# An adaLN block on one core: the second half's down projection as one deep Strassen product

## The chip, the cores and the metric

One core of a Trainium2 chip runs the whole kernel. The metric is device time in microseconds; a profile of one execution gives what each engine did when. TensorE (PE, with its weight loads PEld) multiplies into banks of PSUM, VectorE (DVE) and ScalarE (ACT) read and write PSUM and SBUF, GpSimd (POOL) works on SBUF, and SyncE's queue (SP) issues the DMAs.

## The reference

An adaptive layer norm block on x of 2048 tokens by 512 features, all in float32:

```python
x = x + ga * _A_ref(h, A_wqkv, A_wo)          # linear attention, 32 heads of 16
h = _layernorm(x, axis=-1) * (1 + cb) + sb
g = jnp.einsum("bsd,df->bsf", x, w_gate)      # 512 x 1376
u = jnp.einsum("bsd,df->bsf", x, w_up)        # 512 x 1376
h = g * u
return jnp.einsum("bsf,fd->bsd", h, w_down)   # 1376 x 512
x = x + gb * _B_ref(h, B_w_gate, B_w_up, B_w_down)
```

In `_B_ref` the argument x is the normalized h. The change touches only the last part: the gated product h = g u and its down projection, for half of the tokens.

## The kernel before, in words

**Precision.** Every float32 operand of a matmul is split into a high part in the faster format fp32r and a low part, the rest. A product is three matmuls: high by high, high by low, low by high. The splitting is one copy on ACT (high) and one subtraction on DVE or POOL (low), L196 and L197 in `split`.

**Tiling.** The tokens are four chunks of 512 (four tiles of 128 each, index j), the 1376 hidden features 11 tiles f (ten of 128, and f = 10 of 96). The feed-forward part works on pairs of chunks, (0, 1) and then (2, 3).

**Blocks.** For a pair of chunks and one f, `block` makes g and u of both chunks, a 2x2 by 2x2 block product (chunk and half of the contraction by half of the contraction and gate or up), by Strassen and Winograd's scheme: seven products instead of eight. Each is six matmuls of 128x512 (`times`, L1132), so a block is 42. Four PSUM banks a, b, c, d hold the running sums. ACT copies a bank into another or into SBUF (L1137), DVE adds bank c to p5 after product 5 (L1191) and bank d to u2 after product 6 (L1195), and multiplies g by u for either chunk at the end (`mul`, L1160): the first of these reads bank a, the second bank c. A product can be written to a bank only when the readers of what stood in it are done: product 7 writes bank c after the add of L1191, product 1 of the next block writes bank a. With `aside` a copy of bank a is multiplied; the second pair runs without it.

**Beside the blocks.** `block` is a generator with seven points, after product 1 "p1", 2 "p5", 3 "p6", 4 "p2", 5 "p7", 6 "p3", 7 "p4"; what hangs on a point is issued there, behind whatever its engine has already. These are the loads (L1094) and, on POOL, sums (L1100) and lows (L1118) of the gate and up weights of later blocks, with their highs on ACT (L1111, L1114), the scaling of w_down by gb on DVE (L1277), the split of w_down, the split of h (L196, L197), and work for later chunks by the table `plan`.

**Down projection.** f tiles are taken in groups; `groups` lists for (2, 3): (10, 0, 1), (2, 3, 4), (5, 6, 7), (8, 9). When a group's blocks are through, its matmuls (L1212, L1213, L1214: for each f and token tile high-high, high-low, low-high of 512 columns) are cut into parts, and one part, a down group, is issued after each of the next blocks; DVE adds the result to x (`evac`, L943), and for the last group SP stores it (L945). The last group comes after the last block, its last token tile as two halves of 256 columns. Instructions run in the order in which they are written, engine by engine; a tile framework adds the waits.

## Time and profile before

| what | value |
|---|---|
| median of three runs | 545.67 us (545.53 to 545.91) |
| span of the profiled execution | 543.5 us; 2.2 us less than the median |
| PE busy | 537.6 us, 99% of the span |
| DVE, ACT, POOL busy | 382.4, 293.7, 204.0 us |
| second pair | from 363.67 us to the end |
| one block | 42 matmuls, 9.5 us |

Rows of the timeline read: start in us, duration in us, engine, line, operation, output <- inputs, shapes, count, and in brackets how long the engine had been idle and what released it. Rows of groups read: count, then busy us and mean ns of one, then idle time before them. A matmul row's duration (0.39) is longer than its share of the stream, since matmuls are pipelined; the distance of two starts is what one costs.

### The profile page before, as it was taken

What the parts mean: (1) busy time and instruction counts of PE and PEld (TensorE: products, weight loads), DVE (VectorE), ACT (ScalarE), POOL (GpSimd) and SP (SyncE); (2) the same over time, 40 slices, a digit from 0 to 9 for tenths busy, and PEclk for the clock granted to TensorE, in tenths of its full rate; (3) what the DMA queues carried; (4) which work ended last, traced back from release to release, by engine and by line L of the source; (5) the groups of instructions that cost most, each with busy time, mean ns of one, the idle gap of its engine ahead of it and who ended that gap; (6) DMA issues with size and microseconds to landing.
All of it is one profiled execution on the core that took longest, in us unless ns stands there. A gap on an engine that the chain in (4) does not pass through costs nothing.

```text
span 543.5 us, 7368 instructions
## 1 busy us (share of the span) xinstructions
PE 537.6 (99%) x2419; PEld 441.3 (81%) x2419; DVE 382.4 (70%) x638; ACT 293.7 (54%) x546; POOL 204.0 (38%) x207
## 2 busy tenths in 40 slices
PE   8999999999999999999999999999999999999997
PEld 7888787888888878878888888877888888888885
DVE  7997779999989878769776568985453443444444
ACT  3696776657578765577665545444442344444210
POOL 2001010010021220094896566766666656446100
PEclk9999999999999999999999999999999999999999
DMA  8903326310166165856262151982343222200004
GB/s 285 386 26 112 122 102 209 109 47 2 59 180 206 34 215 168 271 147 184 82 182 86 47 185 40 304 244 63 117 118 92 58 59 59 59 19 1 0 0 157
DMA packets 68455, 65.65 MB, mean 121 GB/s; under 512 B 8448, under 2 KB 46592, under 8 KB 68416
## 3 DMA queue, kind: packets, MB, share of 16 engines
q1 hardware_dynamic: 68416, 65.17, 38.4%
q8 instruction: 19, 0.31, 0.2%
q14 instruction: 20, 0.16, 0.1%
HBM read 46.27 MB, written 18.87 MB: 120 GB/s over the span
## 4 chain that ended last, share of the span: by engine, by line
PE 94%; DVE 3%; SPq 1%; issue 1%; DMA 0%; ACT 0%; DVEq 0%
PE bank L1132 33%; PE acc L873 8%; PE acc L1212 6%; PE acc L1214 6%; PE acc L1213 6%; PE bank L211 4%; PE bank L209 3%; PE bank L210 3%; PE acc L416 2%; PE acc L418 2%; PE bank L958 2%; PE bank L956 2%; PE acc L417 2%; PE bank L957 2%; PE acc L146 2%; SPq L334 1%
## 5 line engine op out<-in xcount | busy, mean ns | idle before, releaser
L1132 PE MATMUL bank<-h,w 128*128 128x512 f32 (+1 forms) x798 | 184.0, 389 | 0.0
L1132 PEld LDWEIGHTS bank<-h,w 128*128 128x128 f32 (+1 forms) x798 | 148.5, 186 | 32.6 <-DVE u L1191 0.2
L1137 ACT ACTIVATE bank<-bank 128x512 f32<-128x512 f32 (+1 forms) x38 | 22.2, 583 | 138.5 <-PE bank L1132 138.3
L943 DVE TENSOR_TENSOR x<-acc,x 128x512 f32<-128x512 f32 (+1 forms) x73 | 48.5, 680 | 49.0 <-PE acc L1214 47.3
L1118 POOL TENSOR_TENSOR w<-raw,w 128x256 fp32r<-128x256 f32 (+3 forms) x38 | 40.4, 1064 | 89.0 <-ACT w L1111 84.9
L197 POOL TENSOR_TENSOR w<-raw,w 128x512 fp32r<-128x512 f32 (+1 forms) x26 | 36.3, 1400 | 65.6 <-ACT w L196 59.9
L1212 PE MATMUL acc<-w,kh 128*128 128x512 f32 (+2 forms) x154 | 59.6, 387 | 0.0
L1213 PE MATMUL acc<-w,kh 128*128 128x512 f32 (+2 forms) x154 | 59.6, 387 | 0.0
L1214 PE MATMUL acc<-w,kl 128*128 128x512 f32 (+2 forms) x154 | 59.5, 386 | 0.0
L265 POOL TENSOR_TENSOR rstd<-ve,half 128x2 f32<-128x2 f32 (+3 forms) x13 | 11.6, 889 | 108.5 <-DVE ve L264 46.0
L1118 POOL TENSOR_TENSOR w<-t,w 128x512 fp32r<-128x512 f32 (+1 forms) x38 | 49.6, 1325 | 0.0
L197 DVE TENSOR_TENSOR kl<-u,kh 128x512 fp32r<-128x512 f32 (+1 forms) x38 | 26.4, 735 | 30.2 <-ACT kh L196 30.2
L211 PE MATMUL bank<-w,h 128*128 128x512 f32 x104 | 40.9, 394 | 0.1
L209 PE MATMUL bank<-w,h 128*128 128x512 f32 x104 | 40.9, 393 | 0.0
L210 PE MATMUL bank<-w,h 128*128 128x512 f32 x104 | 40.6, 390 | 0.0
L873 PE MATMUL acc<-w,xh 128*128 128x512 f32 x120 | 37.1, 390 | 0.0
L1191 DVE TENSOR_TENSOR u<-bank,u 128x512 f32<-128x512 f32 (+1 forms) x19 | 13.1, 688 | 31.3 <-PE bank L1132 23.7
L1212 PEld LDWEIGHTS acc<-w,kh 128*128 128x128 f32 (+1 forms) x154 | 28.9, 188 | 6.0
L1213 PEld LDWEIGHTS acc<-w,kh 128*128 128x128 f32 (+1 forms) x154 | 28.9, 188 | 5.9
L1214 PEld LDWEIGHTS acc<-w,kl 128*128 128x128 f32 (+1 forms) x154 | 28.9, 188 | 5.9
L1100 POOL TENSOR_TENSOR t<-raw,t 128x256 f32<-128x256 f32 (+1 forms) x34 | 25.8, 759 | 2.0 <-DMA raw<-in_B_w_up_dram 0.7
L873 PEld LDWEIGHTS acc<-w,xh 128*128 128x128 f32 x120 | 22.5, 188 | 4.6
(224 smaller groups left out, 1102.2 us busy)
## 6 DMA issues: line engine op xcount, KB each, us to landing
raw<-in_w_mod_dram SPq DMA_DIRECT2D x24, 256.0 KB, 4.0
raw<-in_B_w_down_dram SPq DMA_DIRECT2D x20, 256.0 KB, 3.1
raw<-in_B_w_gate_dram SPq DMA_DIRECT2D x36, 128.0 KB, 3.5
raw<-in_B_w_up_dram SPq DMA_DIRECT2D x36, 128.0 KB, 3.5
x<-in_A_x_dram SPq DMA_DIRECT2D x16, 256.0 KB, 5.4
out_dram<-x SPq DMA_DIRECT2D x15, 256.0 KB, 2.7
moved<-h SPq DMA_DIRECT2D x14, 256.0 KB, 2.2
u<-moved SPq DMA_DIRECT2D x56, 64.0 KB, 2.0
```

The lines of the kernel that those rows point to most:

```text
L197: (low or nc.vector).tensor_tensor(l, src, f32(h), op=ALU.subtract)
L209: nc.tensor.matmul(ps, ah, bh, start=i == 0, stop=False)
L210: nc.tensor.matmul(ps, ah, bl, start=False, stop=False)
L211: nc.tensor.matmul(ps, al, bh, start=False, stop=i == n - 1)
L873: nc.tensor.matmul(yps[i], x, y, start=False, stop=k == KD - 1 and x is al, skip_group_check=True)
L943: nc.vector.tensor_tensor(xt[:, a:b], dn[j][:, a:b], xt[:, a:b], op=ALU.add)
L1100: sub = lambda out, x, y: (on or nc.gpsimd).tensor_tensor(out, x, y, op=ALU.subtract)
L1118: sub = lambda out, x, y: (on or nc.gpsimd).tensor_tensor(out, x, f32(y), op=ALU.subtract)
L1132: mm = lambda x, y, **kw: nc.tensor.matmul(ps, x[:, k], y, skip_group_check=True, **kw)
L1212: nc.tensor.matmul(ps, hh[:, a:b], dh[:n, c:d], start=i == 0, stop=False)
L1213: nc.tensor.matmul(ps, hh[:, a:b], dl[:n, c:d], start=False, stop=False)
L1214: nc.tensor.matmul(ps, hl[:, a:b], dh[:n, c:d], start=False, stop=i == len(hs) - 1)
```

## The change

The four groups of the second pair go. Its 11 blocks run first, with f = 10 first and h kept whole for f = 0 to 9 (`raw`: no split at the end of a block). The first three of them are still followed by the down groups left over from the first pair. Then `Down.run` makes the down projection of both chunks in one: the ten tiles f = 0 to 9 are five pairs, and for a pair, h of two chunks by two tiles times w_down of two tiles by two halves of 256 columns is again a 2x2 by 2x2 product done in seven. The sums over the five pairs stay in PSUM, so that each of the seven products is, for each token tile j, five accumulated pairs. f = 10 is added as an ordinary product (`odd_product`).

The high and low parts of a half of w_down lie side by side in one tile of 512 columns, so that h high by both is one matmul of 512 columns (L1404), and h low by w high one of 256 (L1405); the two halves of the bank are added when it is read (`both`, or `taken`, whose first half is an ACT copy).

The four sums of w_down per pair (`w_sum`, L1352), its scaling (`w_scale`, L1338), seven highs (`w_high`, L1357, ACT) and seven lows (`w_low`, L1362, DVE) hang on the points of the blocks by `planned`; each finished part of 256 KB is parked in device memory and fetched back (`w_park`, `w_fetch`). The sums of h (`h_sum`, L1391) and their splits run partly in the blocks and partly between the seven products. Lines of L1191 and L1195 are now L1194 and L1198, the scaling of f = 10's w_down is L1426 in place of L1277, and the adds on results are L1456.

DVE's order in the first block of the second pair (f = 10), before; raw is w_down, x, u and bank as above:

```order
L197 TENSOR_TENSOR h_4075<-f_3724,h_4074 128x512
L1277 TENSOR_TENSOR raw_3955<-raw_3955,row_1562 96x512
L1191 TENSOR_TENSOR u_4072<-bank_2867,u_4072 96x512
L1195 TENSOR_TENSOR u_4085<-bank_2868,u_4085 96x512
L1160 TENSOR_TENSOR u_4085<-bank_2865,u_4085 96x512
L1160 TENSOR_TENSOR u_4072<-bank_2867,u_4072 96x512
```

and now, where raw_4066 and raw_4068 are w_down of f = 0 and 1, and t their sums:

```order
L197 TENSOR_TENSOR h_4079<-f_3724,h_4078 128x512
L1426 TENSOR_TENSOR raw_3955<-raw_3955,row_1562 96x512
L1338 TENSOR_TENSOR raw_4066<-raw_4066,row_1562 128x512
L1338 TENSOR_TENSOR raw_4068<-raw_4068,row_1562 128x512
L1352 TENSOR_TENSOR t_4100<-raw_4066 128x256
L1352 TENSOR_TENSOR t_4101<-raw_4068,raw_4066 128x256
L1352 TENSOR_TENSOR t_4100<-raw_4068,t_4100 128x256
L1352 TENSOR_TENSOR t_4101<-raw_4068,t_4100 128x256
L1194 TENSOR_TENSOR u_4076<-bank_2867,u_4076 96x512
L1198 TENSOR_TENSOR u_4089<-bank_2868,u_4089 96x512
L1160 TENSOR_TENSOR u_4089<-bank_2865,u_4089 96x512
L1160 TENSOR_TENSOR u_4076<-bank_2867,u_4076 96x512
```

Two scales and four sums now stand between the scaling of f = 10 and the add of bank c (bank_2867). In blocks 10, 12, 14 and 16 (counted from 0 over both pairs, f = 10 is block 8) two scales, four sums and two lows stand ahead of the same add, from point p1 on:

```order
L1362 TENSOR_TENSOR w_4539<-t_4349,w_4539 128x256
L1338 TENSOR_TENSOR raw_4560<-raw_4560,row_1562 128x512
L1338 TENSOR_TENSOR raw_4562<-raw_4562,row_1562 128x512
L1352 TENSOR_TENSOR t_4578<-raw_4560 128x256
L1352 TENSOR_TENSOR t_4579<-raw_4562,raw_4560 128x256
L197 TENSOR_TENSOR kl_4591<-u_4491,kh_4590 128x512
L1352 TENSOR_TENSOR t_4578<-raw_4562,t_4578 128x256
L1352 TENSOR_TENSOR t_4579<-raw_4562,t_4578 128x256
L1194 TENSOR_TENSOR u_4588<-bank_2867,u_4588 128x512
L1198 TENSOR_TENSOR u_4603<-bank_2868,u_4603 128x512
L1160 TENSOR_TENSOR u_4603<-bank_2865,u_4603 128x512
L1160 TENSOR_TENSOR u_4588<-bank_2867,u_4588 128x512
```

Before, only one scaling (L1277) and the two lows of h stood there.

PE at the end of a block of the second pair, before (bank_2867 is bank c, acc a down group's bank):

```order
L1132 MATMUL bank_2867<-h_4011,w_4728 128x512
L1132 MATMUL bank_2867<-h_4074,w_4721 128x512
L1132 MATMUL bank_2867<-h_4075,w_4721 128x512
L1132 MATMUL bank_2867<-h_4074,w_4728 128x512
L1212 MATMUL acc_4873<-w_4486,kh_4543 128x512
L1213 MATMUL acc_4873<-w_4487,kh_4543 128x512
L1214 MATMUL acc_4873<-w_4486,kl_4544 128x512
```

and now, after blocks 11 to 17 (bank_2865 is bank a, the next block's product 1):

```order
L1132 MATMUL bank_2867<-h_4078,w_4520 128x512
L1132 MATMUL bank_2867<-h_4079,w_4520 128x512
L1132 MATMUL bank_2867<-h_4078,w_4527 128x512
L1132 MATMUL bank_2865<-h_3884,w_4630 128x512
L1132 MATMUL bank_2865<-h_3885,w_4630 128x512
L1132 MATMUL bank_2865<-h_3884,w_4630 128x512
L1132 MATMUL bank_2865<-h_3888,w_4630 128x512
L1132 MATMUL bank_2865<-h_3889,w_4630 128x512
```

The down group between the blocks has gone. DVE where the seven products begin, now (kl is the low of a12, the reads of L1456 empty product 1's banks, s_4481 becomes s2):

```order
L1160 TENSOR_TENSOR u_5215<-bank_2865,u_5215 128x512
L1160 TENSOR_TENSOR u_5202<-bank_2867,u_5202 128x512
L197 TENSOR_TENSOR kl_5268<-u_4373,kh_5267 128x512
L197 TENSOR_TENSOR kl_5272<-u_4603,kh_5271 128x512
L197 TENSOR_TENSOR kl_5276<-u_4815,kh_5275 128x512
L197 TENSOR_TENSOR kl_5286<-u_5027,kh_5285 128x512
L197 TENSOR_TENSOR kl_5290<-u_5215,kh_5289 128x512
L1456 TENSOR_TENSOR u_5279<-u_5279,acc_5304 128x256
L1456 TENSOR_TENSOR u_5279<-u_5279,acc_5305 128x256
L1456 TENSOR_TENSOR u_5280<-u_5280,acc_5306 128x256
L1456 TENSOR_TENSOR u_5280<-u_5280,acc_5307 128x256
L1391 TENSOR_TENSOR s_4481<-s_4481,u_4234 128x512
```

Before, DVE had only the adds of L943 after the last block. What stands there on POOL now: s1 and s3 of the fifth pair (L1391), then the lows of s1.

```order
L1391 TENSOR_TENSOR s_5283<-u_5115,u_5202 128x512
L1391 TENSOR_TENSOR u_5115<-u_5127,u_5115 128x512
L197 TENSOR_TENSOR kl_5319<-s_4481,kh_5318 128x512
L197 TENSOR_TENSOR kl_5335<-s_4693,kh_5334 128x512
L197 TENSOR_TENSOR kl_5351<-s_4905,kh_5350 128x512
L197 TENSOR_TENSOR kl_5367<-s_5117,kh_5366 128x512
L197 TENSOR_TENSOR kl_5373<-s_5283,kh_5372 128x512
```

POOL had nothing there before.

The diff, with a few helpers left out:

```diff
--- before.py
+++ after.py
@@ -1147,7 +1147,7 @@
         while todo:
             todo.pop(0)()
 
-    def block(A, R, out, at, aside=False):
+    def block(A, R, out, at, aside=False, raw=False):
 
 
         n, R = R.n, R.of
@@ -1158,7 +1158,10 @@
 
         def mul(ps, x):
             nc.vector.tensor_tensor(x, ps, x, op=ALU.mult)
-            todo.append(lambda: out.append(split_h(x, n)))
+            if raw:
+                out.append(x)
+            else:
+                todo.append(lambda: out.append(split_h(x, n)))
 
         def also(point):
             for do in at.get(point, ()):
@@ -1232,8 +1235,9 @@
         return take
 
     groups = [((0, 1), g) for g in ((0, 1), (2, 3), (4, 5), (6, 7))]
-    groups += [((2, 3), g) for g in ((10, 0, 1), (2, 3, 4), (5, 6, 7), (8, 9))]
     steps = [(cs, f) for cs, g in groups for f in g]
+    LATE = (NF - 1, *range(NF - 1))
+    steps += [((2, 3), f) for f in LATE]
     rights = {}
 
     def right_load(n):
@@ -1261,14 +1265,25 @@
     free = [False]
     parts = []
 
+    def gates(m, cs, A, out, more, raw=False):
+
+        at = {"p7": [lambda: right_load(m + 2), lambda: right_split(m + 1)], "p4": [lambda: right_sums(m + 2)]}
+        for point, does in more.items():
+            at[point] = [*does, *at.get(point, ())]
+        for point in ("p1", "p5", "p6", "p2", "p7", "p3", "p4"):
+            at.setdefault(point, []).append(lambda key=(m, point): [do() for do in plan.pop(key, ())])
+        yield from block(A, rights[m], out, at, aside=not free[0], raw=raw)
+        if free[0] and parts:
+            takes = [down_group(*p) for p in parts.pop(0)]
+            yield
+            for take in takes:
+                take()
+
     def ffn():
 
...
+        wide_down = Down((2, 3), m, draws.pop(m))
+        wide_down.planned()
+        for f in LATE:
+            out = wide_down.h.setdefault(f, [])
+            yield from gates(m, (2, 3), second_side, out, {}, raw=f != LATE[0])
+            m += 1
         flush()
-        while parts:
-            group = parts.pop(0)
-            for p in group:
-                down_group(*p, by_tile=not parts, end=not parts and p is group[-1])()
+        wide_down.run()
+
+    HALF = D // 2
+
+    class Down:
+
...
+        def w_split(self, key, src, low=None):
+            n = src.shape[0]
+            w = B("w", (P, 2, HALF), F32R)[:n]
+            nc.scalar.activation(w[:, 0], src, AF.Copy)
+            (low or nc.vector).tensor_tensor(w[:, 1], src, f32(w[:, 0]), op=ALU.subtract)
+            self.w[key] = w
+
...
+        def w_scale(self, i, *sides):
+            for k in sides:
+                d = self.raw[i][k]
+                nc.vector.tensor_tensor(d, d, gb, op=ALU.mult)
+
...
+        def w_sum(self, i, *names):
+            if i not in self.t:
+                self.t[i] = B("t", (P, 2, HALF)), B("t", (P, 2, HALF))
+            for n in names:
+                x, y = {"t1": ("b12", "b11"), "t2": ("b22", "t1"), "t3": ("b22", "b12"), "t4": ("b21", "t2")}[n]
+                nc.vector.tensor_tensor(self.w_part(i, n), self.w_part(i, x), self.w_part(i, y), op=ALU.subtract)
+
...
+        def w_low(self, i, *names, low=None):
+            for n in names:
+                w = self.w[n, i]
+                (low or nc.vector).tensor_tensor(w[:, 1], self.w_part(i, n), f32(w[:, 0]), op=ALU.subtract)
+
...
+        def h_sum(self, name, *pairs, on=None):
+            for i in pairs:
+                x, y, alu = {"s1": ("a21", "a22", ALU.add), "s3": ("a11", "a21", ALU.subtract),
+                             "s2": ("s1", "a11", ALU.subtract), "s4": ("a12", "s2", ALU.subtract)}[name]
+                own = self.parts.setdefault(i, {})
+                x, y = self.a(i, x), self.a(i, y)
+                to = {"s1": lambda: B("s"), "s3": lambda: y, "s2": lambda: x, "s4": lambda: x}[name]()
+                own[name] = to
+                (on or nc.vector).tensor_tensor(to, x, y, op=alu)
+
...
+        def mm(self, ps, j, pairs, start):
+
+            a, b = j * P, (j + 1) * P
+            for n, ((h, l), w) in enumerate(pairs):
+                k = h.shape[0]
+                nc.tensor.matmul(ps, h[:, a:b], w[:k].rearrange("p t c -> p (t c)"), start=start and n == 0, stop=False, skip_group_check=True)
+                nc.tensor.matmul(ps[:, :HALF], l[:, a:b], w[:k, 0], start=False, stop=False, skip_group_check=True)
+
+        def product(self, ps, j, left, right, start):
+            self.mm(ps, j, [(self.parts[i][left, "split"], self.w[right, i]) for i in range(self.NI)], start)
+
+        def odd_product(self, ps, j, c, half):
+            self.mm(ps, j, [(self.h[LATE[0]][c], self.w["odd", half])], False)
+
...
+        def planned(self):
+
+            def odd_w(half):
+                self.w_split(("odd", half), self.odd[:, half * HALF:(half + 1) * HALF], nc.gpsimd)
+
+            def put(key, *does):
+                plan.setdefault(key, []).extend(does)
+
+            m = self.m
+            put((m, "p6"), lambda: nc.vector.tensor_tensor(self.odd, self.odd, gb[:self.odd.shape[0]], op=ALU.mult))
+            put((m, "p3"), lambda: odd_w(0), lambda: odd_w(1))
+            for i in range(self.NI):
+                first, second, third = m + 2 * i, m + 2 * i + 1, m + 2 * i + 2
+                put((first - 1, "p4") if i else (m, "p1"), lambda i=i: self.w_load(i))
+                at = "p5" if i else "p2"
+                put((first, "p1" if i else "p2"), lambda i=i: self.w_scale(i, 0, 1), lambda i=i: self.w_sum(i, "t1", "t3"))
+                put((first, "p5" if i else "p2"), lambda i=i: self.w_sum(i, "t2", "t4"))
+                put((first, "p2"), lambda i=i: self.w_high(i, "b11", "b21"))
+                put((first, "p3"), lambda i=i: self.w_high(i, "b22", "t1"))
+                put((first, "p4"), lambda i=i: self.w_low(i, "b11", "b21"))
+                put((second, "p1"), lambda i=i: self.w_low(i, "b22", "t1"), lambda i=i: self.w_park(i, "b11", "b21"))
+                put((second, "p2"), lambda i=i: self.w_high(i, "t2", "t3"))
+                put((second, "p3"), lambda i=i: self.w_high(i, "t4"))
+                put((second, "p3"), lambda i=i: self.w_park(i, "b22", "t1"))
+                put((second, "p4"), lambda i=i: self.w_low(i, "t2", "t3"))
+                put((third, "p1"), lambda i=i: self.w_low(i, "t4"), lambda i=i: self.w_park(i, "t2", "t3"))
+                put((third, "p6"), lambda i=i: self.w_park(i, "t4"))
+                put((m + 2 + 2 * i, "p5"), lambda i=i: self.h_split("a11", i))
+                if i + 1 < self.NI:
+                    put((m + 3 + 2 * i, "p5"), lambda i=i: self.h_sum("s1", i), lambda i=i: self.h_sum("s3", i))
+            put((m + 2 * self.NI, "p3"), lambda: self.w_fetch("b11", "b21"))
+            put((m + 2 * self.NI, "p4"), lambda: self.h_split("a12", 0, 1, 2))
+
+        def run(self):
+
...
+            def both(out, ps):
+                add(out, hi(ps))
+                add(out, lo(ps))
+
...
+            def taken(out, ps):
+                copy(out, hi(ps))
+                add(out, lo(ps))
+
+            self.h_sum("s1", self.NI - 1, on=nc.gpsimd)
+            self.h_split("a12", *range(3, self.NI))
+            self.h_sum("s3", self.NI - 1, on=nc.gpsimd)
+            self.w_fetch("t1")
+            one = [acc_bank() for _ in js]
+            for j in js:
+                self.product(one[j], j, "a11", "b11", True)
+                self.h_split("s1", j, low=nc.gpsimd)
+                taken(v[j], one[j])
+            self.drop("a11", "b11")
+            self.h_split("s1", self.NI - 1, low=nc.gpsimd)
+            self.w_fetch("t2")
+            for j in js:
+                self.product(one[j], j, "a12", "b21", False)
+                self.odd_product(one[j], j, 0, 0)
+                self.h_sum("s2", j)
+                self.h_split("s2", j, low=nc.gpsimd)
+                both(x(c0, j, 0), one[j])
+            self.drop("a12", "b21")
+            self.h_sum("s2", self.NI - 1)
+            self.h_split("s2", self.NI - 1, low=nc.gpsimd)
+            self.w_fetch("b22")
+            five = [bank() for _ in js]
+            for j in js:
+                self.product(five[j], j, "s1", "t1", True)
+                self.h_sum("s4", j)
+                self.h_split("s4", j, low=nc.gpsimd)
+                taken(e[j], five[j])
+                add(x(c0, j, 1), e[j], nc.gpsimd)
...
+            six = [acc_bank() for _ in js]
+            for j in js:
+                self.product(six[j], j, "s2", "t2", True)
+                if j == 1:
+                    for k in js:
+                        self.odd_product(five[k], k, 1, 1)
+                self.h_split("s3", j, low=nc.gpsimd)
+                both(v[j], six[j])
+                add(x(c0, j, 1), v[j], nc.gpsimd)
+                if j > 1:
+                    for k in (2 * j - 4, 2 * j - 3):
+                        both(x(c1, k, 1), five[k])
...
+            four = [bank() for _ in js]
+            for j in js:
+                self.product(four[j], j, "a22", "t4", True)
+                self.odd_product(four[j], j, 1, 0)
+                both(x(c1, j, 0), four[j])
+                store(c1, j, 0, HALF)
 
     def fill(n):
         for _ in range(n):
```

109 lines of the change are left out of this document (89 added, 20 removed).

## The prediction

> **What bounds the kernel now.** I read the page first: the busy row, the slices, the chain of work that ended last, the costliest group.
>
> ```profile
> span 543.5 us, 7368 instructions
> ...
> PE 537.6 (99%) x2419; PEld 441.3 (81%) x2419; DVE 382.4 (70%) x638; ACT 293.7 (54%) x546; POOL 204.0 (38%) x207
> ...
> PEclk9999999999999999999999999999999999999999
> ...
> PE 94%; DVE 3%; SPq 1%; issue 1%; DMA 0%; ACT 0%; DVEq 0%
> ...
> L1132 PE MATMUL bank<-h,w 128*128 128x512 f32 (+1 forms) x798 | 184.0, 389 | 0.0
> ```
>
> TensorE is busy 99% of the span at a granted clock that never drops, and 94% of the chain is its matmuls. So a matmul saved is time saved, as long as no new wait appears, and any new wait of TensorE is time lost. The stage that changes begins at 363.67 us. The table by stretches, from there to the last matmul and for one of its blocks, shows PE without a gap, and how much room the others have:
>
> ```profile
> 418.95:428.47 9.52, 9.52 (x43) 7.88 (x42) 4.53 (x8) 5.59 (x11) 3.77 (x4) 1.00 0.29 83
> 363.67:539.67 176.00, 176.00 (x781) 144.47 (x779) 80.92 (x123) 61.81 (x121) 86.26 (x90) 1.00 0.21 60
> ```
>
> The columns are PE, PEld, DVE, ACT, POOL, clock, DMA share, GB/s. DVE works 81 of 176 us. An earlier stretch of the timeline shows what happens when it is late:
>
> ```profile
> 354.97 1.09 DVE L1277 TENSOR_TENSOR raw<-raw,row 128x512 f32<-128x512 f32 x1
> 355.98 0.68 DVE L1191 TENSOR_TENSOR u<-bank,u 128x512 f32<-128x512 f32 x1
> 356.72 1.23 PEld L1132 LDWEIGHTS bank<-h,w 128*128 128x128 f32 x6 [0.20 <-DVE u L1191]
> ```
>
> DVE was held up by the row scaling ahead of the add that frees bank c, so product 7 of that block waited 0.20 us. This is the path on which the change puts much more DVE work.
>
> **Term 1, matmul columns: -6.0.** The pitch comes from starts in the timeline's tail:
>
> ```profile
> 537.63 0.39 PE L1213 MATMUL acc<-w,kh 128*128 128x512 f32 x1
> 537.85 0.39 PE L1214 MATMUL acc<-w,kl 128*128 128x512 f32 x1
> 538.08 0.28 PE L1212 MATMUL acc<-w,kh 128*128 128x256 f32 x1
> 539.39 0.28 PE L1214 MATMUL acc<-w,kl 128*128 128x256 f32 x1
> 539.71 0.42 DVE L943 TENSOR_TENSOR x<-acc,x 128x256 f32<-128x256 f32 x1 [0.29 <-PE acc L1214]
> ```
>
> A 512-column matmul takes 0.2267 us of the stream (the starts are 0.22 to 0.23 apart), a 256-column one 1.31/11 = 0.119, each with a new weight load. The down product of the second pair is now 11 tiles x 8 x 3 = 264 matmuls: 234 of 512 columns, 24 with 96 rows (0.232, from 428.47, 428.71, 428.94 below), and 12 halves of 256. That is 234 x 0.2267 + 24 x 0.232 + 12 x 0.119 = 60.05 us. Afterwards seven products over five pairs and four tiles are 140 matmuls of 512 and 140 of 256, and the odd tile 16 and 16: 140 x 0.3457 + 16 x 0.354 = 54.06 us. The blocks themselves and the first pair's three groups keep their matmuls.
>
> **Term 2, block boundaries: +3.5.** In the second pair the product of bank a by u2 reads bank a itself. One block's end now:
>
> ```profile
> 418.95 9.68 PE L1132 MATMUL bank<-h,w 128*128 128x512 f32 x42
> 426.02 0.69 DVE L1191 TENSOR_TENSOR u<-bank,u 128x512 f32<-128x512 f32 x1 [2.41 <-PE bank L1132]
> 427.38 0.69 DVE L1195 TENSOR_TENSOR u<-bank,u 128x512 f32<-128x512 f32 x1 [0.67 <-PE bank L1132]
> 428.11 1.29 DVE L1160 TENSOR_TENSOR u<-bank,u 128x512 f32<-128x512 f32 x2
> 428.47 0.40 PE L1212 MATMUL acc<-w,kh 96*128 96x512 f32 x1
> 428.71 0.40 PE L1213 MATMUL acc<-w,kh 96*128 96x512 f32 x1
> 428.94 0.39 PE L1214 MATMUL acc<-w,kl 96*128 96x512 f32 x1
> ```
>
> Bank a is free when the first of the two multiplications ends, 428.11 + 0.69 = 428.80, but the matmul stream is through at 428.47. Now a down group fills that hole; after the change the next block's first product, which writes bank a, stands there. A wait for DVE adds about 0.06 to the weight load and some 0.1 more until the matmul runs:
>
> ```profile
> 91.92 1.29 DVE L354 TENSOR_TENSOR h<-f,h 128x512 fp32r<-128x512 f32 x2
> 92.67 0.19 PEld L211 LDWEIGHTS bank<-w,h 128*128 128x128 f32 x1 [0.41 <-DVE h L354]
> 92.67 0.50 PE L211 MATMUL bank<-w,h 128*128 128x512 f32 x1
> ```
>
> So 428.97 - 428.47 = 0.50 us, at the seven boundaries without a down group (blocks 11 to 18): 3.5. A bound below is 0.33 each (2.3), if the wait cost nothing itself.
>
> **Term 3, the first block of the pair (f = 10): +1.5.** There the change issues two scales and four sums, of the first pair of w_down tiles, ahead of the add of bank c.
>
> ```profile
> 363.67 9.83 PE L1132 MATMUL bank<-h,w 128*96 128x512 f32 x42
> 368.49 0.69 DVE L197 TENSOR_TENSOR h<-f,h 128x512 fp32r<-128x512 f32 x1
> 369.10 0.68 DVE L1277 TENSOR_TENSOR raw<-raw,row 96x512 f32<-96x512 f32 x1
> 369.84 0.74 POOL L1118 TENSOR_TENSOR w<-raw,w 128x256 fp32r<-128x256 f32 x1 [4.04 <-ACT w L1111]
> 370.84 0.69 DVE L1191 TENSOR_TENSOR u<-bank,u 96x512 f32<-96x512 f32 x1 [1.07 <-PE bank L1132]
> 372.22 0.69 DVE L1195 TENSOR_TENSOR u<-bank,u 96x512 f32<-96x512 f32 x1 [0.69 <-PE bank L1132]
> ```
>
> From 369.70 on DVE has 2 x 0.61 (the pitch of 368.49 to 369.10) and four of 256 columns, 0.34 to 0.45 each by the 0.42 row above: 1.5. So the add ends not at 371.53 but at about 373.1, and product 7, due when product 6 ends (about 371.95, 0.27 before 372.22), starts at 373.3: +1.35 with DVE undisturbed, 2.5 if POOL's three operations from 369.84 hold it up as below. I take 1.5.
>
> **Term 4, DVE against POOL in blocks 12, 14, 16: +3.6.** The same six operations stand there after product 1 and 2, with a 256-column low before and a 512-column low between them; undisturbed they are 5 us, and the add at about 7.1 us into the block (426.02 - 418.95) would not be late. But POOL now works while they run, which it hardly did before. What that does is seen at 343 to 349 us:
>
> ```profile
> 343.37 1.20 DVE L197 TENSOR_TENSOR h<-s,h 128x512 fp32r<-128x512 f32 x1
> 345.10 1.18 DVE L1050 TENSOR_TENSOR s<-f,s 128x512 f32<-128x512 f32 x1
> 346.20 2.78 DVE L1050 TENSOR_TENSOR s<-f,f 128x512 f32<-128x512 f32 x2
> 343.98 1.75 POOL L1118 TENSOR_TENSOR w<-raw,w 128x512 fp32r<-128x512 f32 x1
> 345.69 1.74 POOL L197 TENSOR_TENSOR w<-raw,w 128x512 fp32r<-128x512 f32 x1
> L1118 POOL TENSOR_TENSOR w<-t,w 128x512 fp32r<-128x512 f32 x18 | 22.9, 1288 | 0.0
> ```
>
> (The last row is the group of 374 to 530 us, where POOL is alone.) A DVE operation with both inputs in SBUF takes 0.69 alone and 1.18 to 1.39 beside POOL; POOL's takes 1.29 alone and 1.75 beside DVE. They take turns: each DVE operation ends about 0.57 after the POOL operation before it and costs POOL 0.46. The Trainium skill ("SBUF — State Buffer", "SBUF: two separate sides") says as much: the port pair shared by VectorE and GpSimd is an exclusive lock for a whole instruction, and a VectorE operation with two SBUF inputs meets it when GpSimd reads SBUF. The trace agrees, with 1.18 in place of 0.69. By the rule's letter a DVE operation can wait for a whole POOL operation, and term 4 would be at its upper bound: 554.9 in place of the sum below.
>
> POOL's other operations, undisturbed, in the groups of the same stretch:
>
> ```profile
> L1118 POOL TENSOR_TENSOR w<-raw,w 128x256 fp32r<-128x256 f32 x9 | 6.7, 742 | 51.3 <-ACT w L1111 51.3
> L1100 POOL TENSOR_TENSOR t<-raw,t 128x256 f32<-128x256 f32 x18 | 13.3, 737 | 0.7
> ```
>
> With no down group between the blocks POOL's four sums (4 x 0.74) fall into the first 3.7 us of a block, and its lows (0.74 + 3 x 1.29 = 4.6) from about 5.9 on. DVE, free of its multiplications at about 0.9, has 4.9 us to do and is locked out for some 2.8 of the sums: ready at 8.6 rather than 5.8, after which lows interfere too. The add then starts at up to 9.0, not 7.1; product 7 is due at 8.16 and needs its result by about 8.0. Start 8.25 to 9.0 means a wait of 0.9 to 1.8 us; the lower bound is 0, if the operations fall into POOL's gaps. I take 1.2 for each of the three. In block 10 a down group stands before, so POOL is through.
>
> **Term 5, in the seven products: +4.4.** 54.06 us of matmuls, 6.9 us for a product of 20 pairs. Product 2 adds into product 1's banks, so it waits until the first has been read. DVE does five lows of a12 before that read, and POOL at the same time s1, s3 and the lows of s1: five turns of 1.29 + 0.46 from about 0.95 put the read's end near 9.0, against 6.9: +2.1 (0 undisturbed: 0.95 + 5 x 0.61 = 4.0). The odd matmuls inside product 4 add into product 3's banks, behind a read that follows DVE's five sums s4 (each against POOL's lows): +1.8; product 5 waits for the last adds on x: +0.5. Undisturbed all this is about +0.3.
>
> **Term 6, the end: +0.45.** The last tile takes two dependent adds of 256 columns (0.42 each) where one stood at 539.71; the store after it is as large as now.
>
> Nothing else is on the path: parks and fetches (35 each of 256 KB) run at a DMA share that was 0.21 and have whole blocks of lead (a w_down load lands in 3.1 us now), ACT has 114 of 176 us free.
>
> **Sum:** -6.0 + 3.5 + 1.5 + 3.6 + 4.4 + 0.45 = +7.45 on the profiled 543.5, so 550.95; the median of 545.67 lies 2.2 above that span, hence **553.1 us**, slower by 1.4%.
>
> **Rivals.** (a) *POOL and DVE do not meet*: stretched operations are few, since each fits a gap. Terms 4 and 5 shrink to 0.3 and term 3 to 1.35: -6.0 + 3.5 + 1.35 + 0.3 + 0.45 = -0.4, 545.3. For it: POOL's groups of 374 to 530 us show no stretch at all (1288, 737); against it: DVE then had 0.68 us of such work between the multiplications and the add, now about 5. (b) *Faster*: the columns are all that counts, and the waits shrink as well, because queues run ahead (for it: one wait of 0.20 us where DVE was late); -6.0 + 0.45 with a third of terms 2 and 3 is -3.9, 541.8; with none, 540.1. Against it stands the gap of 428.47 to 428.80, which nothing fills. (c) *The lock binds throughout*: over two blocks POOL needs 2 x (2.9 + 4.6) = 15 us, and 16 DVE operations with two SBUF inputs take 0.25 to 0.46 each from it, 5 to 6: 20 to 21 of 20. From the point where this passes the blocks' own time POOL's lows come late for product 2 or 3, and each of four pairs loses up to 1.5 more: 557 to 559.
>
> **How the numbers follow.** Forecast 0.52 (548 to 556); (c) 0.12; (a) 0.15, of which a little falls on either side of no change; (b) 0.2. A measurement of this kernel tells 0.2% (1.1 us) from nothing: faster 0.22, same 0.13, slower 0.65. The range takes in (a) and most of (c) and cuts the best of (b): 542.5 to 558; the forecast's own is 548 to 556.
>
> **What would show it.** PE busy down by about 6 us, its idle time up by 13, in rows: weight loads of the blocks waiting about 0.5 for the multiplication of bank a (seven times); one wait of 1.3 to 2.5 in the block of 96-column weights; waits for the add of bank c in every second block, with DVE sums above 0.42 and POOL lows above 1.29 beside them; the second product's first matmul late by 2 us. If DVE's rows keep 0.42 and 0.69, (a) holds. A 256-column matmul that costs more than 0.12 beside a 512-column one, or a fetch that lands late, would prove the sum wrong elsewhere.

## The result, and the profile after

The changed kernel takes 550.61 us (549.22 to 551.37, four runs) against 545.6 us (545.11 to 545.91): 1.0088 of the time before, with a 95% interval of 1.0071 to 1.0105. Slower, as forecast; 553.1 was said, 2.5 us too much. One run of an experiment (899.28 us, at a mean clock of 0.557) and one of the kernel before (1934.74 us) lie far above all others and are left out of the comparisons. The page of the profile after (an execution of 551.37 us):

```profile
span 549.3 us, 7863 instructions
...
PE 537.5 (98%) x2461; PEld 440.2 (80%) x2461; DVE 442.9 (81%) x734; ACT 311.9 (57%) x595; POOL 242.8 (44%) x231
...
PE   8999999999999999999999999998999999989897
...
PE 87%; DVE 9%; issue 2%; ACT 1%; SPq 1%; DMA 0%; DVEq 0%; ACTq 0%
```

DVE has gone from 3% to 9% of the chain, PE from 94% to 87%: waits for DVE have come into the path. The waits view from 360 us on (columns: total us, times, longest) names them:

```profile
PEld bank L1132 <- issue: 4.3, 7, 0.7
...
PEld bank L1132 <- DVE u L1194: 2.8, 4, 1.9
...
PEld bank L1404 <- DVE u L1456: 1.8, 1, 1.8
PEld acc L1404 <- DVE u L1456: 1.8, 1, 1.8
```

The seven waits put down to "issue" are the seven block boundaries without a down group; the PE rows of the timeline give the releaser of the four longest, the multiplication of bank a:

```profile
405.39 9.68 PE L1132 MATMUL bank<-h,w 128*128 128x512 f32 x42
415.37 19.91 PE L1132 MATMUL bank<-h,w 128*128 128x512 f32 x84 [0.30 <-DVE u L1160]
435.58 19.88 PE L1132 MATMUL bank<-h,w 128*128 128x512 f32 x84 [0.30 <-DVE u L1160]
455.76 19.89 PE L1132 MATMUL bank<-h,w 128*128 128x512 f32 x84 [0.30 <-DVE u L1160]
```

Two blocks take 20.2 us where 2 x 9.52 = 19.04 are matmuls. In the block of f = 10, and in the seven products:

```profile
373.97 1.63 PE L1132 MATMUL bank<-h,w 128*96 128x512 f32 x6 [1.40 <-DVE u L1194]
...
494.31 0.50 PE L1404 MATMUL acc<-w,kh 128*128 128x512 f32 x1 [1.49 <-DVE u L1456]
...
515.91 0.50 PE L1404 MATMUL bank<-w,kh 96*128 96x512 f32 x1 [1.48 <-DVE u L1456]
```

Laid against the terms of the prediction, from the starts of the stages in both traces (before: second pair 363.67, last matmul done 539.51, end 543.49; after: 364.12, end of the block of f = 10 375.44, block 11 at 405.39, products 485.61, last matmul done 545.35, end 549.30):

| part | predicted | measured |
|---|---|---|
| matmul columns (term 1) | -6.0 | -5.5 |
| boundaries, and late adds in blocks 12, 14, 16 (terms 2, 4) | +3.5 and +3.6 | +4.1 together |
| block of f = 10 (term 3) | +1.5 | +1.65 |
| waits in the seven products (term 5) | +4.4 | +5.2, of which 1.6 is a halved clock |
| end (term 6) | +0.45 | 0.0 |
| before the second pair | 0 | +0.45 |
| sum on the profiled span | +7.45 | +5.8 |

Terms 2 and 4: blocks 11 to 18 take 485.61 - 405.39 = 80.22 us, 4.06 more than 8 x 9.52. The product stage takes 59.74 us; one later version ran it with one gap of 0.38 in 54.92, so its matmuls are 54.5, and 5.2 is waiting or a slower clock. The 0.45 before the stage was there by 252 us and arose in the first ten microseconds, where nothing was changed.

### The profile page after: what moved, and what is told of

It is laid out like the page before. It is cut to its first block, busy times and chain, and to the rows that moved or that the text cites. A ratio compares the mean times of both kernels' runs of the same rounds, so it can differ in the third digit from the quotient of the medians.

```text
span 549.3 us, 7863 instructions
## 1 busy us (share of the span) xinstructions
PE 537.5 (98%) x2461; PEld 440.2 (80%) x2461; DVE 442.9 (81%) x734; ACT 311.9 (57%) x595; POOL 242.8 (44%) x231
## 4 chain that ended last, share of the span: by engine, by line
PE 87%; DVE 9%; issue 2%; ACT 1%; SPq 1%; DMA 0%; DVEq 0%; ACTq 0%
PE bank L1132 31%; PE acc L873 7%; PE bank L211 3%; PE bank L209 3%; PE bank L210 3%; PE acc L1215 3%; PE acc L1217 3%; PE acc L1216 3%; PE acc L1404 2%; PE bank L1404 2%; PE acc L416 2%; PE bank L958 2%; PE acc L418 2%; PE bank L956 2%; PE acc L417 2%; PE bank L957 2%
## 5 line engine op out<-in xcount | busy, mean ns | idle before, releaser
L197 POOL TENSOR_TENSOR w<-raw,w 128x512 fp32r<-128x512 f32 (+1 forms) x15 | 22.1, 1482 | 53.4 <-ACT w L196 47.8
L943 DVE TENSOR_TENSOR x<-acc,x 128x512 f32<-128x512 f32 x40 | 26.4, 685 | 7.9 <-PE acc L1217 6.2
L1404 PE MATMUL acc<-w,kh 128*128 128x512 f32 x84 | 31.1, 410 | 1.5 <-DVE u L1456 1.5
L196 ACT ACTIVATE kh<-u 128x512 fp32r<-128x512 f32 (+1 forms) x43 | 24.6, 623 | 10.6 <-DVE u L1391 8.1
L1100 POOL TENSOR_TENSOR t<-raw,t 128x256 f32<-128x256 f32 (+1 forms) x34 | 28.4, 835 | 2.1 <-DMA raw<-in_B_w_up_dram 0.9
L1137 ACT ACTIVATE u<-bank 128x512 f32<-128x512 f32 (+2 forms) x44 | 25.2, 572 | 6.9 <-PE bank L1132 6.8
L1194 DVE TENSOR_TENSOR u<-bank,u 128x512 f32<-128x512 f32 (+1 forms) x19 | 13.0, 686 | 19.2 <-PE bank L1132 15.1
L1404 PE MATMUL bank<-w,kh 128*128 128x512 f32 (+1 forms) x72 | 25.5, 395 | 1.5 <-DVE u L1456 1.5
L416 PE MATMUL acc<-kh,xh 128*128 128x512 f32 x64 | 25.2, 394 | 0.0
L418 PE MATMUL acc<-kl,xh 128*128 128x512 f32 x64 | 25.0, 391 | 0.0
```

The costliest lines, as they stand in the source:

```text
L197: (low or nc.vector).tensor_tensor(l, src, f32(h), op=ALU.subtract)
L416: nc.tensor.matmul(tacc[k], xh[:, a:b], kh, start=first, stop=False)
L418: nc.tensor.matmul(tacc[k], xh[:, a:b], kl, start=False, stop=last)
L1100: sub = lambda out, x, y: (on or nc.gpsimd).tensor_tensor(out, x, y, op=ALU.subtract)
L1137: nc.scalar.activation(out, x, AF.Copy)
L1404: nc.tensor.matmul(ps, h[:, a:b], w[:k].rearrange("p t c -> p (t c)"), start=start and n == 0, stop=False, skip_group_check=True)
```

## The experiments

All edits are of the changed kernel unless the text says otherwise. Ratios are to the kernel before. Line numbers move by a few in the edited kernels: L1194 is also L1196 or L1200, L1456 also L1459, L1463 or L1464, and so on. What an edit saves is counted from the median of 550.61. Two of its four runs have a lower mean clock (last section); the two others are 549.22 and 549.95, so a saving can be too large by about 1 us.

**POOL's reading, at the start of the seven products.**

```diff
-                (on or nc.vector).tensor_tensor(to, x, y, op=alu)
+                if on is not None:
+                    on.memset(to, 0.0)
+                    continue
+                (on or nc.vector).tensor_tensor(to, x, y, op=alu)
...
+                if name == "s1":
+                    nc.scalar.activation(h, self.a(i, name), AF.Copy)
+                    nc.gpsimd.memset(f32(l), 0.0)
```

> The changed kernel, but POOL's work at the start of the seven products (s1 and s3 of the fifth pair, the five lows of s1) only fills its outputs with zeros, so it reads nothing from SBUF; those parts of the sum are left out. DVE's five lows of a12 stay. If it is POOL's reading that stretches them (lock): each falls from 1.49 us to about 0.69, the read of product 1's banks starts near 490 rather than 493.85 by the changed kernel's clock, and TensorE's wait of 1.75 us before product 2 is gone. If the five lows are simply too much work ahead of that read, or the read waits for ScalarE's copy, the wait stays at 1.75 us.

546.66 us, 1.0026 (1.0015 to 1.0036). DVE's rows of the changed kernel and of this one:

```profile
486.45 7.47 DVE L197 TENSOR_TENSOR kl<-u,kh 128x512 fp32r<-128x512 f32 x5
493.85 1.40 DVE L1456 TENSOR_TENSOR u<-u,acc 128x256 f32<-128x256 f32 x4
```

```profile
486.19 3.09 DVE L197 TENSOR_TENSOR kl<-u,kh 128x512 fp32r<-128x512 f32 x5
489.20 0.75 DVE L1463 TENSOR_TENSOR u<-u,acc 128x256 f32<-128x256 f32 x2
```

The same five lows take 7.47 us beside POOL's sums and lows (the first 0.68, the four others 1.76 to 1.79) and 3.09 here, and the wait before product 2 is gone. The fills, however, come earlier than the sums and lows whose place they take, and the last of them ends at 485.2, before the first low:

```profile
482.79 2.41 POOL L1401 MEMSET kl<- 128x512 f32 x5 [3.02 <-issue]
```

So POOL is idle beside the lows. The run shows that POOL's work stretches them, not their number; whether it is POOL's reading it cannot show (the fills in the blocks, below, do). Not expected: the wait inside product 4 shrank from 1.8 to 0.4 as well, though nothing was changed there.

**The a12 splits earlier.**

```diff
-            put((m + 2 * self.NI, "p4"), lambda: self.h_split("a12", 0, 1, 2))
+            put((m + 2 * self.NI, "p6"), lambda: self.h_split("a12", 0, 1, 2))
```

> The changed kernel, with the splits of a12 of the first three pairs one product earlier than the end of the last block (after its third product rather than its seventh), where POOL has nothing to do. Two lows instead of five stand before the read of product 1's banks. Both the lock and too much work say: the wait before product 2 goes from 1.75 to 0, 548.9 in place of 550.6; the lock says besides that the three early lows take 0.69 each. If the read waits for ScalarE's copy instead, the wait stays.

546.58 us, 1.0021 (1.0011 to 1.0030): 4.0 us less, where 1.75 was expected (3.0 less than the two runs of the changed kernel at full clock). The timeline of DVE:

```profile
481.85 1.90 DVE L197 TENSOR_TENSOR kl<-u,kh 128x512 fp32r<-128x512 f32 x3 [1.17 <-ACT kh L196]
483.67 0.68 DVE L1194 TENSOR_TENSOR u<-bank,u 128x512 f32<-128x512 f32 x1
...
486.70 2.38 DVE L197 TENSOR_TENSOR kl<-u,kh 128x512 fp32r<-128x512 f32 x2
489.01 0.41 DVE L1456 TENSOR_TENSOR u<-u,acc 128x256 f32<-128x256 f32 x1
```

Three lows take 1.90 us with POOL idle, two take 2.38 beside it (0.68 and 1.78); the read begins at 489.01, and both waits in the products are gone (0.2 us is left). Here, as with the fills, the second wait went with the first. That it is only DVE's backlog of the first, carried through two products, does not follow: with all edits (below) one execution has the second wait without the first. A new wait of 0.64 us came into the weight loads of the last block, whose add at 483.67 now stands behind the three lows.

**Product 1 in a bank of its own in every second block.**

```diff
+        if own is not None:
+            a = own[:n]
...
-        yield from block(A, rights[m], out, at, aside=not free[0], raw=raw)
+        yield from block(A, rights[m], out, at, aside=not free[0], raw=raw,
+                         own=acc_bank() if m in (11, 13, 15, 17) else None)
```

> The changed kernel, with product 1 of every second block from 11 on in a PSUM bank of the down groups' pool, which is idle there, so that the next block's first product never writes the bank that the multiplication still reads. If the wait at the seven boundaries is for bank a: 7 x 0.49 = 3.4 us less, 547.2. If DVE is the bound there, the wait moves to the add of bank c in the middle of the blocks (0.2 us three times now) or to product 2's bank, and little is won (under 1 us).

551.43 us, 1.0113 (1.0098 to 1.0128): nothing won. The boundaries are without a wait, and the add of bank c is late instead, by 2.0 us in each of blocks 12, 14 and 16:

```profile
424.47 1.24 PEld L1132 LDWEIGHTS bank<-h,w 128*128 128x128 f32 x6 [2.02 <-DVE u L1196]
445.43 1.23 PEld L1132 LDWEIGHTS bank<-h,w 128*128 128x128 f32 x6 [2.00 <-DVE u L1196]
466.37 1.22 PEld L1132 LDWEIGHTS bank<-h,w 128*128 128x128 f32 x6 [2.01 <-DVE u L1196]
```

Two blocks now take 445.43 - 424.48 = 20.95 us, more than the 20.2 with the boundary waits. The rows ahead of the add, first of the changed kernel, then of this one, show where the rest comes from:

```profile
421.76 1.30 DVE L1352 TENSOR_TENSOR t<-raw,t 128x256 f32<-128x256 f32 x2
422.99 0.68 DVE L1194 TENSOR_TENSOR u<-bank,u 128x512 f32<-128x512 f32 x1
...
421.85 0.93 POOL L1118 TENSOR_TENSOR w<-raw,w 128x256 fp32r<-128x256 f32 x1 [1.84 <-ACT w L1111]
```

```profile
421.44 2.38 DVE L1355 TENSOR_TENSOR t<-raw,t 128x256 f32<-128x256 f32 x2
423.74 0.68 DVE L1196 TENSOR_TENSOR u<-bank,u 128x512 f32<-128x512 f32 x1
...
421.08 1.04 POOL L1118 TENSOR_TENSOR w<-raw,w 128x256 fp32r<-128x256 f32 x1 [1.39 <-ACT w L1111]
422.07 2.88 POOL L1118 TENSOR_TENSOR w<-t,w 128x512 fp32r<-128x512 f32 x2
```

ScalarE's highs follow TensorE, and POOL's lows follow the highs. With no wait at the boundary they come 0.77 us earlier, on top of DVE's last two sums, which take 2.38 instead of 1.30. The boundary wait had been covering that.

**The same with t2 and t4 behind the add.**

```diff
-                put((first, "p5" if i else "p2"), lambda i=i: self.w_sum(i, "t2", "t4"))
+                put((first, "p4" if i else "p2"), lambda i=i: self.w_sum(i, "t2", "t4"))
```

> The alternating bank of product 1, and besides the last two sums (t2, t4) of each pair of w_down tiles from the second on are issued after the last multiplication of their block, no longer ahead of the add of bank c. If the late add (2.0 us of wait in blocks 12, 14, 16 with the alternating bank alone) comes from DVE's work ahead of it: those waits fall to 0.3 or less, and two blocks take 19.1 to 19.4 us rather than 20.95: 5 us less than with the alternating bank alone, 546.4. If DVE has simply too much to do in two blocks, the wait moves on to bank d or to the next block, and the time stays near 551.

547.23 us, 1.0029 (1.0019 to 1.0039), 4.2 less than without it. The waits for the add are 0.43, 0.60 and 0.57 in the weight loads, two blocks take 19.5 us (432.90 to 452.41, 452.41 to 471.92), a little over what was expected. These waits are no longer in blocks 12, 14 and 16 but in 13, 15 and 17, where t2 and t4 now come ahead of the next add: a part of the wait has moved on by one block, as the other branch of the expectation had it, and most of it is gone. So it was mainly what stood ahead of the add, not the sum of DVE's work: DVE does the same operations.

**POOL's reading in the blocks**, with the alternating bank and the changed kernel's order on DVE.

```diff
+            if on == "fill":
+                sub = lambda out, x, y: nc.gpsimd.memset(out, 0.0)
...
-..."p4": [lambda: right_sums(m + 2)]}
+..."p4": [lambda: right_sums(m + 2, "fill" if m > 10 else None)]}
```

(and the lows in the same way)

> The alternating bank with the order of the changed kernel on DVE; but POOL's sums and lows of the gate and up weights of blocks 12 (13 for sums) to 18 only fill their outputs with zeros, so POOL reads nothing there; those parts of the weights are left out. If POOL's reading is what holds DVE (lock): DVE's scales fall from 1.19 to 0.69, its sums and lows to 0.42, the 2.0 us waits for the add of bank c go, two blocks take 19.1 us, 546. If the number of DVE operations is the cause, they stay at 2.0 us and the time at 551.

546.1 us, 1.0009 (0.9999 to 1.0019), 5.3 less than the alternating bank alone. No wait for bank c is left after block 8. DVE's groups of 405 to 486 us, with the alternating bank alone and here:

```profile
L1365 DVE TENSOR_TENSOR w<-t,w 128x256 fp32r<-128x256 f32 x16 | 12.9, 848 | 0.0
L1341 DVE TENSOR_TENSOR raw<-raw,row 128x512 f32<-128x512 f32 x6 | 7.1, 1226 | 0.0
L1355 DVE TENSOR_TENSOR t<-raw,t 128x256 f32<-128x256 f32 x6 | 7.0, 1172 | 0.1
```

```profile
L1370 DVE TENSOR_TENSOR w<-t,w 128x256 fp32r<-128x256 f32 x16 | 6.6, 452 | 0.0
L1346 DVE TENSOR_TENSOR raw<-raw,row 128x512 f32<-128x512 f32 x6 | 3.9, 686 | 0.0
L1360 DVE TENSOR_TENSOR t<-raw,t 128x256 f32<-128x256 f32 x6 | 2.5, 423 | 0.1
```

The same operations, 27.0 us in one and 13.0 in the other. Most of them have POOL idle beside them here, since the fills are short. But 20 of DVE's operations with two SBUF inputs ran at least 0.1 us beside a fill, and they kept 0.42 us (11 of 256 columns) and 0.69 (nine of 512), as with POOL idle; beside POOL's sums and lows the same shapes take 0.85 and 1.22 in the mean in the changed kernel. One such place:

```profile
407.70 0.68 DVE L1399 TENSOR_TENSOR s<-u,u 128x512 f32<-128x512 f32 x1
408.41 0.69 DVE L1399 TENSOR_TENSOR u<-u,u 128x512 f32<-128x512 f32 x1
...
407.44 1.72 POOL L1122 MEMSET w<- 128x256 f32 x4
```

So it is POOL's reading that stretches them.

**The first pair's scales and sums later.** Two places were tried. Right behind the add of bank c:

```diff
-                put((first, "p1" if i else "p2"), lambda i=i: self.w_scale(i, 0, 1), ...
-                put((first, "p5" if i else "p2"), lambda i=i: self.w_sum(i, "t2", "t4"))
+                put((first, "p1" if i else "p7"), lambda i=i: self.w_scale(i, 0, 1), ...
+                put((first, "p5" if i else "p7"), lambda i=i: self.w_sum(i, "t2", "t4"))
...
-                put((first, "p2"), lambda i=i: self.w_high(i, "b11", "b21"))
+                put((first, "p2" if i else "p3"), lambda i=i: self.w_high(i, "b11", "b21"))
```

> The changed kernel, with the two scales and four sums of the first pair of w_down issued after the add of bank c in the block of f = 10 rather than before. If they are what makes that add late: the wait of 1.86 us of the weight load of product 7 there goes, 1.65 us less, 548.9. If they only move the wait to the next reader (the add of bank d, and through it the next block), part of it comes back there, up to 1.65; the down group between should hide it.

550.55 us, 1.0096 (1.0081 to 1.0111): nothing won. The wait has moved to the next block:

```profile
371.97 2.71 DVE L1338 TENSOR_TENSOR raw<-raw,row 128x512 f32<-128x512 f32 x2
374.59 1.52 DVE L1352 TENSOR_TENSOR t<-raw 128x256 f32<-128x256 f32 x1
376.03 0.95 DVE L1352 TENSOR_TENSOR t<-raw,raw 128x256 f32<-128x256 f32 x1
376.91 1.83 DVE L1352 TENSOR_TENSOR t<-raw,t 128x256 f32<-128x256 f32 x2
378.66 0.68 DVE L1198 TENSOR_TENSOR u<-bank,u 96x512 f32<-96x512 f32 x1
...
380.20 2.08 PE L1132 MATMUL bank<-h,w 128*128 128x512 f32 x8 [2.02 <-DVE u L1160]
```

The six operations take 6.7 us beside POOL's lows instead of 2.7, the add of bank d and the multiplications come that much later, and the 4.1 us of the down group do not cover it. And behind the multiplications, with t2, t4 and the highs there too and the first lows in the next block:

```diff
-..."p1" if i else "p2"), lambda i=i: self.w_scale(i, 0, 1), lambda i=i: self.w_sum(i, "t1", "t3"))
+..."p1" if i else "p4"), lambda i=i: self.w_scale(i, 0, 1), lambda i=i: self.w_sum(i, "t1", "t3"))
...
-                put((first, "p4"), lambda i=i: self.w_low(i, "b11", "b21"))
+                put((first, "p4") if i else (second, "p1"), lambda i=i: self.w_low(i, "b11", "b21"))
```

> The changed kernel, with the scales and sums of the first pair of w_down, and their highs, behind the two multiplications that end the block of f = 10, and two of their lows in the next block. Then nothing of it stands ahead of the add of bank c, of bank d or of the multiplications: the 1.65 us of that block go and nothing comes back, since the down group's results are not needed for 13 us: 548.9. If DVE is simply short of time there, the add of bank c in the next block is late instead (four lows and two lows of h stand ahead of it).

548.29 us, 1.0049 (1.0035 to 1.0062): 2.3 less, 1.3 less than the runs at full clock, and no wait in blocks 8 to 10.

**The odd matmuls of product 4 one tile later**, alone.

```diff
-                if j == 1:
+                if j == 2:
```

> The changed kernel with that edit alone. If the wait before product 4's odd matmuls is a wait of its own: 1.75 us less, 548.9, and the wait before product 2 stays at 1.75. If the adds behind it (product 3's results, needed by product 5) are the limit, the wait moves there and the time stays at 550.6.

550.13 us, 1.0088 (1.0073 to 1.0103): no change. The wait before these matmuls is gone, and product 5 waits 2.02 us:

```profile
520.49 0.47 PE L1404 MATMUL bank<-w,kh 128*128 128x512 f32 x1 [2.02 <-issue]
```

**Together**: alternating bank, t2 and t4 late, the first pair's work behind the multiplications, the a12 splits after the last block's first product ("p1" where the edit above had "p6").

> Alternating bank, t2 and t4 late, the first pair's scales and sums late, and the splits of a12 of three pairs already after the last block's first product. If the waits are independent once DVE is ordered like this: 550.6 - 4.0 (measured for the early splits) - 3.45 - 0.63 (boundaries and adds) - 1.65 = 540.9, faster than the kernel before by 4.4. If DVE and POOL are the bound together, something near 545.

541.84 us, 0.9933 (0.9921 to 0.9945): faster than both kernels, by 3.7 us than before and 8.8 than the changed one, though 0.9 above what independent waits would have given. Its waits from 405 us to the products:

```profile
431.06 10.75 PEld L1132 LDWEIGHTS bank<-h,w 128*128 128x128 f32 x48 [0.41 <-DVE u L1196]
450.56 10.75 PEld L1132 LDWEIGHTS bank<-h,w 128*128 128x128 f32 x48 [0.59 <-DVE u L1196]
470.06 10.79 PEld L1132 LDWEIGHTS bank<-h,w 128*128 128x128 f32 x48 [0.59 <-DVE u L1196]
482.69 0.19 PEld L1407 LDWEIGHTS acc<-w,kh 128*128 128x128 f32 x1 [0.34 <-DMA w<-down_b]
```

Its times have two levels: 541.72 to 541.88 four times, 543.44 and 543.93. The profile is of the highest, and has a wait of 1.57 us before product 4's odd matmuls, although the wait before product 2 is gone:

```profile
510.07 0.51 PE L1407 MATMUL bank<-w,kh 96*128 96x512 f32 x1 [1.57 <-DVE u L1459]
```

So these were moved in it too:

> As the version with all four edits, and the odd matmuls into product 3's banks one token tile later within product 4 (after its third tile rather than its second), 1.73 us later. If the second level of that version's times (543.4 to 543.9 beside 541.7 to 541.9) is the wait of 1.73 us before these matmuls, as in its profile, the high level goes, and all times lie within 0.5 us of 541.8 or a little below. If the levels come from the clock or from elsewhere, both stay.

542.0 us, 0.9938 (0.9926 to 0.9951). The expectation failed: five runs lie at 541.54 to 542.26 and one at 543.8. Its profile is of the lower level, with one gap of 0.38 us in the seven products, so it does not show by itself where the 1.7 us of the other level lie; the last section lays it beside the profile of the higher level.

## Why the prediction was right

**Term 1** held: -5.5 against -6.0. Matmuls of 512 and 256 columns side by side cost what their rows cost before, each with a new weight load.

**Term 3** held: +1.65 against +1.5. The experiment with the work behind the multiplications took 1.3 to 2.3 off, by which runs of the changed kernel it is counted from.

**Term 2** held: of the 4.06 us of blocks 11 to 18, the starts of the matmuls put 0.17 on each of the three late adds (their weight loads wait 0.32 to 0.33), 0.5 in all, which leaves 3.5 for seven boundaries, 0.50 each as forecast.

**Term 4** is the one that was mis-sized: 3.6 was said, 0.5 measured. The mechanism is as forecast, DVE's scales took 1.22 us each and its lows 0.84 to 0.92 beside POOL. But the working let POOL's lows reach the last two sums, and in the changed kernel they reach only the last: POOL's sums end at 420.0, its lows begin at 421.85, and DVE does three operations undisturbed between. The add started 7.6 us into the block, not 8.25 to 9.0. The alternating bank shows besides that terms 2 and 4 are not independent: each boundary wait put TensorE half a microsecond back against DVE's queue, and when the waits were taken away, the late add grew from 0.17 to 1.9 us (20.95 - 19.04) for each of the three blocks. A price of one that is worked out without the other cannot be added to it.

**Term 5** had the right sizes (1.75 against 2.1, 1.75 against 1.8) for the two waits. Its five turns from 0.95 make 9.7 as they are written, not 9.0; 9.0 comes out when the first low is free, and so it was: 0.68 for the first, 1.76 to 1.79 for the four others, and the add on which product 2 waited done 8.65 us into the stage. The cause of the first wait is shown: with POOL idle beside the lows it goes. What the second is worth alone is not: it went with the first in two versions, stood without it in one execution, and removing it alone moved it on to product 5. In the profiles it goes with a pattern of turns between DVE and POOL (last section). A further 1.6 us in the profiled execution was the clock (below), which no term had.

**Term 6** was wrong: the last two adds take 0.88 us where one took 0.42, but from the last matmul to the end it is 3.95 us against 3.98. The store after them ended sooner; why was not tried.

**Luck.** That the total is only 2.5 us off is in part luck: against the 3.1 too much of term 4 stands 1.6 us of halved clock that was not forecast. And one sign failed: PE's busy time did not fall by 6 us (537.6 and 537.5), and its idle time rose by 5.9, not 13. A matmul's row is 0.39 us long at a distance of 0.227, so 0.16 us of every wait counts as busy, and so does the time at half clock.

**The rivals.** (a), DVE and POOL do not meet, falls with the fills in the blocks: 27.0 us of DVE operations against 13.0. (b), faster, did not happen with the changed kernel; reordered, and with the second bank, the same matmuls came to 541.84. That this is (b)'s 541.8 is chance, since the waits left there are not a third of each. (c), the lock binds throughout, did not happen: from 360 us on TensorE has no wait that is put down to POOL. What the Trainium skill ("SBUF — State Buffer", "Who interferes with whom") states, that VectorE with two SBUF inputs contends with a GpSimd instruction that reads SBUF and not with one that only writes, agrees with the fills in the blocks: 0.42 and 0.69 us beside a fill, 0.85 and 1.22 beside POOL's reads.

## What to carry to other kernels

A wait that is worked out for one engine and a wait for the same engine a few microseconds later are not to be added: work out the first, shift everything behind it by it, and then ask whether the second is still there. Where VectorE and GpSimd both read SBUF, put VectorE's operations with two SBUF inputs behind the operation on which TensorE waits, not ahead of it, and count them at nearly double (0.85 for 0.42, 1.22 for 0.69 here). When an edit removes a wait and the time stays, look for the same wait at the next reader (the add of bank c, product 5, the next block): three of the edits here did just that, and only the order of the whole queue, together with the second bank, brought the gain.

## What was not expected of the hardware

TensorE's clock halved in the middle of the kernel. In the profiled execution, behind the second wait of 1.5 us, the table by stretches gives (last columns: clock, DMA share, GB/s):

```profile
515.00:516.00 1.00, 0.09 (x1) 0.09 (x1) 0.56 (x2) 0.41 (x2) 0.84 (x2) 1.00 0.07 27
516.00:517.00 1.00, 1.00 (x4) 0.86 (x5) 1.00 (x2) 0.00 (x0) 1.00 (x2) 0.66 0.00 0
517.00:518.00 1.00, 1.00 (x5) 0.90 (x4) 0.96 (x4) 0.93 (x2) 0.85 (x2) 0.50 0.00 0
518.00:519.00 1.00, 1.00 (x5) 0.80 (x5) 0.57 (x2) 1.00 (x3) 1.00 (x1) 0.50 0.00 0
519.00:520.00 1.00, 1.00 (x5) 0.86 (x5) 0.17 (x1) 1.00 (x3) 1.00 (x2) 0.63 0.00 0
```

A pair of matmuls took 0.64 us instead of 0.35 for 3.3 us, which costs 1.6. Two of the four runs have a mean clock of 0.997 and 0.995 (551.37 and 551.27 us), the two with 1.000 are 549.22 and 549.95: the spread of the changed kernel is about this much. The wait of the same length 22 us earlier had no such effect. The profile with the alternating bank and t2 and t4 late has the same stretch at 0.50 behind the same wait (513.25 us, 1.49 idle); four other profiles with both waits do not have it. Of the seven versions with the wait before product 2, 12 of 36 runs have a mean clock of 0.997 or less; of the four without it, none of 30. The Trainium skill ("TensorE: Matmul & The Clock Gate", "Part 1: The HAM clock gate (the "warmup" mystery)") puts the loss of full speed behind at least one idle window of about 3.4 us, taken on a free-running clock. Here 1.5 us of idleness were followed by it in two profiles, and in others not. That the position in such a window decides is not shown by these runs.

The turns of DVE and POOL can fall into two patterns for the same instructions. In product 3 the low of POOL took 1.75 us and DVE's sum 1.10 with the a12 splits early, and 1.29 and 1.27 with all edits, where POOL's add on x took 1.18 instead of 0.73; a cycle is 2.4 us in one and 2.6 in the other. In every profile the second wait goes with the pattern. With cycles of 2.6 the last of DVE's five sums ends 14.2 to 14.3 us after the start of product 3, and the wait is there: in the changed kernel, in the six other versions that keep the wait before product 2 (in one of them before product 5), and in the execution of 543.93 us with all edits. With cycles of 2.4 it ends at 12.4 to 12.7, and at most 0.4 is left: with the fills at the start of the products, with the a12 splits early, and in the execution of 541.6 us with the odd matmuls moved as well. So the two levels of the last version's times are most likely these two patterns; the moved odd matmuls could not end that, since alone they only moved the wait to product 5. One profile of each level, of two versions that differ by one edit, is all there is for it. What tips the turns into one pattern or the other stays open.
